# Joins of a triangular inverse in four corners, u transposed in one pass, and loads in halves at two positions, in a chunked attention with a gated MLP

## The chip, the core and the metric

The kernel runs on one core of a Trainium2 chip, in one launch. The metric is device time in microseconds. TensorE multiplies matrices into PSUM, VectorE (DVE), ScalarE (ACT) and GpSimd (POOL) work elementwise, and SyncE (SP) issues almost all DMAs. Each engine works through its own instructions in the order in which the program issues them, and waits on semaphores for the others.

## The reference, cut to what matters

Inputs: r, k, v, w, a, b of shape (4, 8, 768, 40), and the MLP's weights. A state of 40x40 per batch and head runs over 768 steps:

```
y[t]  = r[t] @ state
Sa    = state @ a[t]
state = state * w[t] - outer(Sa, b[t]) + outer(v[t], k[t])
```

y, with the heads side by side (width 320), goes through a gated MLP: `h = gelu(x @ w_in)` with 1024 columns, halves u and v, v normalised and mixed over time by a 768x768 matrix, and `x + (u * v) @ w_out`.

## The kernel before, in words

The recurrence is cut into 12 chunks (`c`) of 64 steps. In a chunk the steps depend on each other through a unit lower triangular 64x64 matrix for each of the 32 batch-head pairs; its inverse turns the chunk into matrix products. Work is done per chunk and half (`f` = 0, 1, two batches each).

The stages of one chunk, with lines of the listing:

- **gate** (338 to 397): VectorE scans the decays from tile `main` (two buffers, loaded by `load_main`, line 274), scales k, a and b, TensorE transposes (`kt`) and multiplies (`ab`, 384 to 386, on four tiles of 64x64, two PSUM banks), VectorE and ScalarE mask the results into `at` and `nts`.
- **inverse** (399 to 478): the 32x32 diagonal blocks of the inverse come from a substitution on GpSimd for two chunks at a time (`inv_load` copies a unit pattern out of `band`, `inv_sub` 415, `inv_end`, `inv_turn`, `inv_back`). The lower left corner is joined from them by two rounds of small matmuls: `inv_g` (452) writes PSUM tile `gp`, `post_g` (461) copies it to `gs`, `inv_x` (466) writes `xp`, `post_x` (475) copies it into `xt`. A round has 16 entries q and two halves h: 32 matmuls of 64 rows by 32 columns, each half on one tile of the array; a float32 matmul shows as two records in the trace.
- **chain** (499 to 633): with the state: `chain1` (`ru`), `chain2` (`us`), `post2` (u into the lower half of `vu`), `chain3` (`sp`, the new state), `copy3` (state to `vs`), `chain_u` (573, u transposed, `ut`), `post_u` (into `vut`), `chain4` (`pq`, from `rt` and `vut`), `chain5` (`yp`), `post5` and `store5` (y to DRAM tensor `xd`). `chain_t` transposes the state for `chain5` (`tp`).
- **loads**: `load_main`, `load_vb` (v for `chain1`), `load_vu` (a ScalarE copy into `vu`, 485) and `load_rv` (492, r and v transposed, into `rt` and `vut`) for later chunks, all on SyncE but `load_vu`.
- **fill** (911 to 945): parts of the MLP of earlier steps are done inside the attention, by loads of `xf` out of `xd`, a product `hf` and a store `hd`.

Every piece of work has a position in microseconds (constants `YC`, `CHAIN`, `YG`, `GATE`, `BACK` and others, lines 45 to 78; `at_` at 639). `in_order` (123) sorts the pieces by position and holds back those that would need a PSUM bank too early; the pieces are then issued in this order. The positions therefore set only the order on each engine and queue; the real times follow from waits. After chunk 11 the rest of the MLP runs.

Of the kernel before, what the change touches and what calls it, by code (L numbers as in the profile page):

```python
# [9 lines left out]
F32 = mybir.dt.float32  # L10
# [6 lines left out]
B, H, S, D = 4, 8, 768, 40  # L17
C = 64
NCH = S // C
NP = H // 2  # L20
DM = H * D
# [5 lines left out]
NQ = B * NP  # L27
# [13 lines left out]
LOADS = -12.0  # L41
PER = 25.258
LATE = 2.5
STORE = 1.5
GATE = ((-101.908, -100.107, -99.028, -96.184, -97.801, -95.604, -92.188, -90.251, -93.577, -91.478, -91.823),
    (-93.163, -92.271, -89.673, -85.987, -88.462, -85.151, -80.147, -78.616, -83.325, -79.712, -81.287))
GATE0 = {(0, 0): (-50.0, (0, 0.6, 1.2, 2.0, 2.1, 3.5, 5.0, 6.2, 6.1, 10.6, 7.4)), (0, 1): (-43.168, (-2.368, -1.768,
# [159 lines left out]
def engines(tc):  # L207
    nc = tc.nc
    return tuple(InOrder(tc, e) for e in (nc.vector, nc.scalar, nc.gpsimd, nc.tensor, nc.sync))
# [6 lines left out]
def attention(tc, a, xd, flag, keep, ps, mlp=None):  # L216
# [3 lines left out]
    V, A, G, T, Q = engines(tc)  # L220
    with ExitStack() as ctx:

        def pool(nm, side):

            c = ctx.enter_context(ExitStack())
            return c.enter_context(tc.tile_pool(name=nm, bufs=1, side=side)), c.close

        mlp.open_fill()
        st, _ = pool("at_static", "left")
# [4 lines left out]
        gt, gt_right = pool("at_gate", "right")  # L234
# [7 lines left out]
        def static(nm, n, shape, where=None):  # L242
            return [(where or st).tile(shape, F32, name=f"{nm}{i}") for i in range(n)]
# [6 lines left out]
        xts = static("xt", 2, [128, NQ, C])  # L250
        spare = gt.tile([128, 1], F32, name="spare")
        ident = st.tile([128, 128], F32, name="ident")
        mask = st.tile([128, C], F32, name="mask")
        band = st.tile([128, 128], F32, name="band")
        n = WU
        ones, rc, hsp = fixed[0][:, 0:n], fixed[0][:, n - C:2 * n - C], fixed[1][:, 0:n]
        nts = [p.tile([128, 2, NQ, C], F32, name=f"nts{i}") for i, p in enumerate((iw, iv))]
# [3 lines left out]
        gss = static("gs", 1, [128, 16, 32], iv)  # L261
        scs = static("sc", 2, [128, 2 * NP, C])
        rts = static("rt", 2, [128, 2, 4, C])
        call = keep.tile([128, NCH * B, NP], F32, name="call")
        vuts = static("vut", 2, [128, 2, 2, 4, C])
        vus = static("vu", 2, [128, 2 * DM + 24])

        exs = ring("ex", [128, 2, NP, C + 1])
        ats = ring("at", [128, 2, NP, 2, C], RING_AT)
# [1 line left out]
        def main_of(i):  # L271
            return mains[i % 2]

        def load_main(i):
            if i < 2 * NCH:
                for h in range(2):
                    Q.dma_start(out=main_of(i)[64 * h:64 * h + D], in_=a["main"][i, D * h:D * h + D])

        warm = gt.tile([128, 128], F32, name="warm")
        V.memset(warm, 0.0)  # L280
# [26 lines left out]
        def blanks():  # L307
            out = []
            for t in gss + scs:
                out.append(lambda t=t: G.memset(t, 0.0))  # L310
            for t in kbts:
                out.append(lambda t=t: G.memset(t[:, :, DM:DM + 24], 0.0))
            for t in vus:
                out.append(lambda t=t: G.memset(t[64:128, 2 * DM:2 * DM + 24], 0.0))
            return out

        def zeros():
# [15 lines left out]
        def nt_of(c):  # L333
            return nts[c // 2 % 2][:, c % 2]

        gate, kbs, unit, x1_of, st2, pqt, bk, xin, yts = {}, {}, {}, {}, {}, {}, {}, {}, {}
# [107 lines left out]
        def inv_back(c, k):  # L444
# [3 lines left out]
            else:  # L448
                r = slice(64 * (k - 1), 64 * (k - 1) + 32)
                A.copy(out=xt[r, :, 0:32], in_=xt[r, :, 32:64])  # L450

        def inv_g(c):
            nt, x1z = nt_of(c), x1_of[c]
            gp = bk["gp"] = ps("gp")
            for q in range(NQ):
                for h in range(2):
                    r = 64 * h
                    T.matmul(gp[r + 32:r + 64, 32 * q:32 * q + 32], lhsT=nt[r:r + 64, q, 32:64],
                             rhs=x1z[r:r + 64, q], start=True, stop=True, tile_position=(r, r + 32))

        def post_g(c):
            gs, gv = gss[0], bk.pop("gp").rearrange("p (q x) -> p q x", x=32)
            A.copy(out=gs[32:64], in_=gv[32:64])
            A.copy(out=gs[96:128], in_=gv[96:128])

        def inv_x(c):
            xt, gs = xts[c % 2], gss[0]
            xp = bk["xp"] = ps("xp")
            for q in range(NQ):
                for h in range(2):  # L470
                    r = 64 * h
                    T.matmul(xp[r:r + 32, 32 * q:32 * q + 32], lhsT=gs[r:r + 64, q],
                             rhs=xt[r:r + 64, q, 32:64], start=True, stop=True, tile_position=(r, r))

        def post_x(c):
            xt, xv = xts[c % 2], bk.pop("xp").rearrange("p (q x) -> p q x", x=32)
            A.copy(out=xt[0:32, :, 32:64], in_=xv[0:32])
            A.copy(out=xt[64:96, :, 32:64], in_=xv[64:96])


        def load_vb(c, f):
            if c < NCH:
                Q.dma_start(out=vss[f][0:64], in_=a["vb"][c, f])

        def load_vu(c, f):
            if c == 0:
                Q.dma_start(out=vus[f][0:64, 0:2 * DM], in_=a["vs"][0, f])
            elif c < NCH:
                A.copy(out=vus[f][0:64, 0:2 * DM].rearrange("p (g h x d) -> p g h x d", g=4, h=2, x=2),
                       in_=vss[f][0:64].rearrange("p i (g x) h d -> p (i g) h x d", x=2))  # L490

        def load_rv(c, f):
            if c < NCH:
                for x in range(2):
                    r = slice(64 * x, 64 * x + D)
                    Q.dma_start(out=rts[f][r], in_=a["rt"][c, f, x])
                    Q.dma_start(out=vuts[f][r, 0], in_=a["vt"][c, f, x])

        def chain1(c, f):
            at, vs = at_of(c, f), vss[f]  # L500
# [13 lines left out]
            return scs[f][:, :, 0:D]  # L514

        def vu_of(f):
            return vus[f][:, 0:2 * DM].rearrange("p (i g h x d) -> p i g h x d", i=2, g=2, h=2, x=2)

        def chain_t(c, f):
            if c:  # L520
# [20 lines left out]
        def post2(c, f):  # L541
            us, vu = bk.pop(("us", f)), vu_of(f)
            for h in range(2):
                for x in range(2):
                    A.mul(out=vu[64:128, :, :, h, x], in_=us[h][64 * x:64 * x + 64, 0:160].rearrange("p (i g d) -> p i g d", i=2, g=2), mul=-1.0)
# [26 lines left out]

        def chain_u(c, f):
            ut = bk["ut", f] = ps("ut")
            for j in range(16):
                r = 64 * (j % 2)
                T.matmul(ut[r:r + 64, C * (j // 2):C * (j // 2) + C], lhsT=vus[f][64:128, D * j:D * j + 64],
                         rhs=ident[64:128, 64:128], start=True, stop=True, tile_position=(64, r), skip_group_check=True)

        def post_u(c, f):  # L580
            e, ut = 64 + D, bk.pop(("ut", f))
# [53 lines left out]
        for f in range(2):  # L635
            load_vu(0, f)
        pieces = []

        def at_(p, f, *args, **kw):
            pieces.append((p, f, args, kw))  # L640

        for k, f in enumerate(blanks()):
            at_(BLANKS + 0.01 * k, f)
        for k, f in enumerate(zeros()):
            at_(ZEROS + 0.01 * k, f)
        for f in range(2):
            at_(LOADS, load_vb, 0, f)
            at_(LOADS, load_rv, 0, f)
        for c in range(NCH):
            for f in range(2):  # L650
                y, n = GATE0.get((c, f)) or (YG[c], GATE[f])
                at_(y + n[0], gate_1, c, f, 0)
                at_(y + n[1], gate_1, c, f, 1)
                at_(y + n[2], gate_2, c, f, E={"V": V, "G": G}[GATEE.get((c, f), GE)[0]])
                at_(y + n[3], gate_c, c, f)
                for i in range(2):
                    at_(y + n[4 + i], gate_3, c, f, i, E={"V": V, "G": G}[GATEE.get((c, f), GE)[1]])
                for g, p in zip((gate_t, gate_k, gate_s), n[6:]):
                    at_(y + p, g, c, f)
                for h in range(2):  # L660
                    at_(y + n[9] + 0.001 * h, gate_a, c, f, h)
                    at_(y + n[10] + 0.001 * h, gate_n, c, f, h)
                at_(y + n[5] + LATE, load_main, 2 * c + f + 2)
                z, n = YC[c], CHAIN0.get((c, f), CHAIN[f])
                for g, p in zip((chain1, post1, chain_t, post_t, chain2, post2, chain3, post3, copy3, chain_u, post_u, chain4, post4, chain5, post5), n):
                    at_(z + p, g, c, f)
                at_(z + n[14] + STORE, store5, c, f)
                at_(z + n[0] + LATE, load_vb, c + 1, f)
                at_(z + max(n[6], n[9]) + LATE, load_vu, c + 1, f)
                at_(z + n[13] + LATE, load_rv, c + 1, f)  # L670
            z = YC[c]
            for (g, *k), p in zip(((inv_back, 0), (inv_back, 1), (inv_back, 2), (inv_g,), (post_g,), (inv_x,), (post_x,)), BACK0.get(c, BACK)):
                at_(z + p, g, c, *k)
        for g in GROUPS:
            z, v = (0, INV0[g[0]]) if g[0] in INV0 else (YC[g[0]], INV)
            at_(z + v[0], inv_load, g)
            at_(z + v[1], inv_in, g)
            for s in range(31 - LAST):
                y = {}
# [601 lines left out]
```

## Time and profile before

| | us |
|---|---|
| median of three runs | 648.37 |
| lowest and highest | 646.72, 649.48 |
| profiled execution, its own time | 651.27 |
| its span in the trace | 649.5 |
| TensorE matmul busy, share of the span | 551.1, 85% |
| VectorE, GpSimd, ScalarE busy | 496.9, 370.0, 363.6 |
| mean granted share of TensorE's clock | 0.899 |

All times in the trace count from the start of the span. The time of an execution is a little longer than its span. A row of the chain names what the last work waited for, back to the start: start, duration and what; "issue" is time in which the engine waited for nothing that the profile shows. A row of a timeline or of the chain that merges records gives their number after an x.

### The profile page before, as it was taken

Reading aid. Unit: us, or ns where it says so; the run is one execution under the profiler, and the core shown is the slowest. Engines: PE = TensorE matmul, PEld = TensorE weight load, DVE = VectorE, ACT = ScalarE, POOL = GpSimd, SP = SyncE. Lnnn points to the kernel's source line nnn. Section 1 sums busy time; section 2 is a strip of 40 time slices with the busy share of each in tenths; the row PEclk is TensorE's granted clock in tenths of the full one; section 3 lists DMA queues with packets and bytes.
Section 4 is the critical chain, followed back from the end, with each engine's and each line's share of the span. In section 5 each row is a group of like instructions: output and inputs, shape, how many; then the busy total and the mean of one; then the engine's idle time right before and its main releaser. Section 6 shows DMA issues by size and latency. Waiting matters only on the chain.

```text
span 649.5 us, 25246 instructions
## 1 busy us (share of the span) xinstructions
PE 551.1 (85%) x10734; PEld 502.6 (77%) x10734; DVE 496.9 (77%) x954; ACT 363.6 (56%) x769; POOL 370.0 (57%) x600
## 2 busy tenths in 40 slices
PE   6438859768998798999998799698998998899896
PEld 5327758657887787888887687597998987899896
DVE  7767989699779566877799856748699799778943
ACT  3333957457877576787867678556345324625410
POOL 3485838816974844588389642656644632544331
PEclk8658877567999897999998899788999999999999
DMA  5443334243444353553354346337023541401001
GB/s 194 130 120 94 96 80 117 77 121 89 128 113 134 91 151 92 154 131 108 105 137 134 106 133 168 106 113 203 14 80 104 157 144 67 124 26 56 30 13 55
DMA packets 54945, 69.69 MB, mean 107 GB/s; under 512 B 21704, under 2 KB 39752, under 8 KB 52808
## 3 DMA queue, kind: packets, MB, share of 16 engines
q1 hardware_dynamic: 54824, 67.99, 36.8%
q8 instruction: 86, 1.41, 1.0%
q14 instruction: 35, 0.29, 0.1%
HBM read 54.86 MB, written 13.11 MB: 105 GB/s over the span
## 4 chain that ended last, share of the span: by engine, by line
PE 46%; DVE 26%; issue 10%; POOL 7%; ACT 6%; DMA 2%; SPq 1%; DVEq 0%; POOLq 0%; ACTq 0%
PE sg L202 7%; PE yp L202 5%; PE hf L202 4%; PE op L202 3%; DVE v L202 3%; PE sp L202 3%; PE ab L202 3%; PE pq L202 3%; PE ut L202 3%; PE ru L202 3%; DVE stg L202 3%; PE hu L202 3%; PE kt L202 2%; PE xp L202 2%; DVE p L202 2%
## 5 line engine op out<-in xcount | busy, mean ns | idle before, releaser
L202 POOL TENSOR_TENSOR tg<-x,n 128x135 f32<-128x135 f32 (+25 forms) x203 | 106.2, 523 | 98.1 <-ACT gs L202 40.0
L202 POOL TENSOR_TENSOR x<-x,tg 128x135 f32<-128x135 f32 (+25 forms) x203 | 108.2, 533 | 15.9
L202 PE MATMUL sg<-wsh,vh 128*128 128x384 f32 x192 | 65.9, 343 | 4.6 <-DVE y L202 3.9
L202 PE MATMUL sg<-wsh,vl 128*128 128x384 f32 x192 | 66.0, 344 | 3.5 <-POOL vl L202 3.5
L202 PE MATMUL sg<-wsl,vh 128*128 128x384 f32 x192 | 65.8, 343 | 1.7 <-DVE wsl L202 0.9
L202 ACT ACTIVATE nts<-ab 32x512 f32<-32x512 f32 x96 | 46.5, 484 | 28.2 <-PE ab L202 27.0
L202 PE MATMUL kt<-ident,kb 128*128 128x128 f32 x192 | 35.4, 333 | 27.4 <-DVE fixed L202 17.8
L202 POOL TENSOR_TENSOR gx<-g,gy 128x384 fp32r<-128x384 f32 x30 | 32.0, 1076 | 40.1 <-ACT gy L202 40.1
L202 PEld LDWEIGHTS kt<-ident,kb 128*128 128x128 f32 x192 | 26.7, 170 | 32.6 <-issue 26.7
L202 DVE TENSOR_TENSOR at<-ab,mask 64x512 f32<-64x512 f32 x48 | 31.8, 677 | 26.1 <-ACT nts L202 25.4
L202 POOL TENSOR_TENSOR rs<-rs,mhalf 128x1 f32<-128x1 f32 x24 | 14.7, 615 | 64.9 <-DVE rs L202 61.3
L202 ACT CAST vh<-v 128x512 fp32r<-128x512 f32 x24 | 14.6, 620 | 58.3 <-DVE v L202 58.3
L202 PE MATMUL ab<-at,kb 64*64 64x64 f32 x1536 | 39.6, 269 | 7.1 <-DVE fixed L202 6.2
L202 PEld LDWEIGHTS ab<-at,kb 64*64 64x64 f32 x1536 | 35.7, 179 | 10.1 <-issue 8.4
L202 ACT CAST gy<-g 128x384 fp32r<-128x384 f32 x30 | 15.3, 513 | 50.2 <-DVE g L202 50.2
L202 PEld LDWEIGHTS sg<-wsh,vh 128*128 128x128 f32 x192 | 36.5, 190 | 5.9 <-issue 2.6
L202 PEld LDWEIGHTS sg<-wsh,vl 128*128 128x128 f32 x192 | 36.6, 191 | 5.4 <-POOL vl L202 5.4
L202 PE MATMUL yp<-pqs,kbt 128*64 128x64 f32 x768 | 33.5, 249 | 7.8 <-ACT vs L202 3.4
L202 PEld LDWEIGHTS yp<-pqs,kbt 128*64 128x64 f32 x768 | 29.5, 159 | 11.6 <-ACT vs L202 3.6
L202 PEld LDWEIGHTS sg<-wsl,vh 128*128 128x128 f32 x192 | 36.5, 190 | 2.3 <-DVE wsl L202 1.2
L202 PE MATMUL sp<-vu,kbt 128*64 128x40 f32 x704 | 28.1, 237 | 11.6 <-issue 8.7
L202 DVE SCALAR_TENSOR_TENSOR g<-sg,gl,bt 128x384 f32<-128x384 f32 x32 | 19.5, 610 | 23.9 <-POOL gx L202 14.9
(158 smaller groups left out, 1609.2 us busy)
## 6 DMA issues: line engine op xcount, KB each, us to landing
main<-main SPq DMA_DIRECT2D x44, 321.4 KB
hd<-hv SPq DMA_DIRECT2D x20, 256.0 KB
v<-hd SPq DMA_DIRECT2D x20, 256.0 KB
vs<-vb SPq DMA_DIRECT2D x24, 160.0 KB
rt<-rt SPq DMA_DIRECT2D x48, 80.0 KB
vut<-vt SPq DMA_DIRECT2D x48, 80.0 KB
xd<-yt SPq DMA_DIRECT2D x96, 40.0 KB
ws<-seq_w SPq DMA_DIRECT2D x20, 192.0 KB
```

What stands on the lines that cost most here:

```text
L202: return self.tc.keep_in_program_order(f(*a, **k))
```

## The change

It has four parts. `inv_g` and `inv_x` put the entries q = 0 to 7 (`f` = 0) and 8 to 15 (`f` = 1) onto different columns of the array, so that consecutive matmuls go to four tiles; the PSUM tile has 256 columns instead of 512, and the posts copy it in four pieces of 32 partitions by 256 instead of two of 32 by 512. `chain_u` transposes two heads at a time out of a `vu` whose heads lie 64 apart instead of 40: 8 transposes instead of 16 matmuls. The two halves of a `main` load get positions of their own (from chunk 2 on, the second 4.6 or 3.4 later), and so do the two halves of a load of r and v (1.7 or 1.15 later). For the wider `vu`, `band` moves to the pool of the gate, and more of `vu` is cleared at the start.

```diff
+MAIN_GAP = (4.6, 3.4)
+RV_GAP = (1.7, 1.15)
...
-        band = st.tile([128, 128], F32, name="band")
+        band = gt.tile([128, 128], F32, name="band")
...
-        vus = static("vu", 2, [128, 2 * DM + 24])
+        vus = static("vu", 2, [128, 64 * 15 + D])
...
-        def load_main(i):
+        def load_main(i, h):
             if i < 2 * NCH:
-                for h in range(2):
-                    Q.dma_start(out=main_of(i)[64 * h:64 * h + D], in_=a["main"][i, D * h:D * h + D])
+                Q.dma_start(out=main_of(i)[64 * h:64 * h + D], in_=a["main"][i, D * h:D * h + D])
...
-                out.append(lambda t=t: G.memset(t[64:128, 2 * DM:2 * DM + 24], 0.0))
+                out.append(lambda t=t: G.memset(t[64:128, 0:960].rearrange("p (j x) -> p j x", x=64)[:, :, D:64], 0.0))
...
+        def corners():
+            return [(8 * f + j, 64 * h + 32 * f, 64 * h) for j in range(8) for f in range(2) for h in range(2)]
+
         def inv_g(c):
...
-            for q in range(NQ):
-                for h in range(2):
-                    r = 64 * h
-                    T.matmul(gp[r + 32:r + 64, 32 * q:32 * q + 32], lhsT=nt[r:r + 64, q, 32:64],
-                             rhs=x1z[r:r + 64, q], start=True, stop=True, tile_position=(r, r + 32))
+            for q, n, r in corners():
+                T.matmul(gp[n:n + 32, 32 * (q % 8):32 * (q % 8) + 32], lhsT=nt[r:r + 64, q, 32:64],
+                         rhs=x1z[r:r + 64, q], start=True, stop=True, tile_position=(r, n), skip_group_check=True)
 
         def post_g(c):
-            gs, gv = gss[0], bk.pop("gp").rearrange("p (q x) -> p q x", x=32)
-            A.copy(out=gs[32:64], in_=gv[32:64])
-            A.copy(out=gs[96:128], in_=gv[96:128])
+            gs, gv = gss[0], bk.pop("gp")[:, 0:256].rearrange("p (q x) -> p q x", x=32)
+            for f in range(2):
+                for r in (0, 64):
+                    A.copy(out=gs[r + 32:r + 64, 8 * f:8 * f + 8], in_=gv[r + 32 * f:r + 32 * f + 32])
...
+        def heads(f, r):
+            e = vus[f][r, 0:1]
+            return bass.AP(tensor=e.tensor, offset=e.offset, ap=[e.ap[0], [64, 16], [1, D]])
...
-        def load_rv(c, f):
+        def load_rv(c, f, x):
             if c < NCH:
-                for x in range(2):
-                    r = slice(64 * x, 64 * x + D)
-                    Q.dma_start(out=rts[f][r], in_=a["rt"][c, f, x])
-                    Q.dma_start(out=vuts[f][r, 0], in_=a["vt"][c, f, x])
+                r = slice(64 * x, 64 * x + D)
+                Q.dma_start(out=rts[f][r], in_=a["rt"][c, f, x])
+                Q.dma_start(out=vuts[f][r, 0], in_=a["vt"][c, f, x])
...
         def chain_u(c, f):
             ut = bk["ut", f] = ps("ut")
-            for j in range(16):
-                r = 64 * (j % 2)
-                T.matmul(ut[r:r + 64, C * (j // 2):C * (j // 2) + C], lhsT=vus[f][64:128, D * j:D * j + 64],
-                         rhs=ident[64:128, 64:128], start=True, stop=True, tile_position=(64, r), skip_group_check=True)
+            for j in range(8):
+                T.transpose(out=ut[0:64 + D, C * j:C * j + C], identity=ident[64:128, 64:128],
+                            in_=vus[f][64:128, 128 * j:128 * j + 64 + D])
...
-                at_(y + n[5] + LATE, load_main, 2 * c + f + 2)
+                for h in range(2):
+                    at_(y + n[5] + LATE + (MAIN_GAP[f] if h and c > 1 else 0), load_main, 2 * c + f + 2, h)
...
-                at_(z + n[13] + LATE, load_rv, c + 1, f)
+                for x in range(2):
+                    at_(z + n[13] + LATE + (RV_GAP[f] if x else 0), load_rv, c + 1, f, x)
```

`inv_x` and `post_x` change as `inv_g` and `post_g` do; `load_vu` and the operands of `post2` and `chain3` address `vu` through `heads`.

## Rows read from the trace of the kernel before

**Rows 1.** Busy time by stretch: us, each engine's busy time (records), PEclk, DMA share, GB/s

```profile
64.00:150.00 86.00, 64.21 (x1726) 57.58 (x1720) 74.86 (x151) 54.20 (x118) 50.66 (x98) 0.72 0.37 99
...
278.00:304.00 26.00, 24.02 (x740) 21.11 (x735) 17.62 (x34) 18.84 (x41) 22.85 (x37) 1.00 0.46 121
...
424.00:650.00 226.00, 207.34 (x1150) 197.97 (x1142) 169.81 (x315) 89.97 (x176) 103.40 (x96) 0.98 0.27 83
```

**Rows 2.** The chain that ended last, 150 to 320 us: start, us, what

```profile
161.51 0.45 PE us L202 x32
...
170.94 1.13 PE gp L202 x64
...
174.47 1.12 issue
...
192.32 1.67 PE yp L202 x64
194.00 0.93 PE ab L202 x64
...
217.82 3.78 issue
...
221.93 1.90 PE ut L202 x32
223.83 2.93 PE yp L202 x64
226.76 1.67 PE ab L202 x64
...
248.17 2.54 issue
...
281.05 1.08 PE ut L202 x32
...
294.93 1.31 issue
...
302.24 1.02 PE kt L202 x8
```

**Rows 3.** The page: busy by engine; the instruction DMA queue: packets, MB, share

```profile
PE 551.1 (85%) x10734; PEld 502.6 (77%) x10734; DVE 496.9 (77%) x954; ACT 363.6 (56%) x769; POOL 370.0 (57%) x600
...
q8 instruction: 86, 1.41, 1.0%
```

**Rows 4.** Timeline of SyncE's DMA issues, 120 to 300 us

```profile
212.96 0.71 SPq L202 DMA_DIRECT2D main<-main  x2
213.84 0.48 SPq L202 DMA_DIRECT2D vs<-vb  x1
...
242.88 0.71 SPq L202 DMA_DIRECT2D main<-main  x2
245.81 0.47 SPq L202 DMA_DIRECT2D vs<-vb  x1
```

**Rows 5.** Busy time by stretch, around the piece of issue at 217.82

```profile
213.00:219.00 6.00, 4.81 (x187) 4.41 (x183) 5.54 (x13) 4.80 (x13) 5.45 (x8) 1.00 0.78 191
222.00:228.00 6.00, 6.00 (x152) 5.76 (x156) 2.20 (x5) 1.28 (x2) 5.37 (x9) 0.50 0.04 8
```

**Rows 6.** The chain that ended last, 320 to 440 us

```profile
394.23 0.58 ACT gs L202
...
395.46 1.20 PE xp L202 x62
...
401.83 1.21 PE ut L202 x32
```

**Rows 7.** The chain that ended last, 60 to 150 us

```profile
65.82 0.58 ACT gs L202
...
91.61 1.92 PE gp L202 x64
```

**Rows 8.** Groups by shape, ScalarE: busy us, mean ns, idle before

```profile
L202 ACT ACTIVATE nts<-ab 32x256 f32<-32x256 f32 x48 | 18.1, 378 | 0.6
...
L202 ACT COPY gs<-gp 32x512 f32<-32x512 f32 x24 | 13.9, 578 | 0.6
```

**Rows 9.** Timeline, 231 to 237 us

```profile
233.21 1.18 ACT L202 COPY gs<-gp 32x512 f32<-32x512 f32 x2
...
234.57 0.88 PE L202 MATMUL xp<-xt,gs 64*32 64x32 f32 x44
```

More of the change, by code (lines that the diff above doesn't have):

```diff
@@ L468, in inv_x @@
             xp = bk["xp"] = ps("xp")
[L469 to L473, printed above, removed]
+            for q, n, r in corners():
+                T.matmul(xp[n:n + 32, 32 * (q % 8):32 * (q % 8) + 32], lhsT=gs[r:r + 64, q],
+                         rhs=xt[r:r + 64, q, 32:64], start=True, stop=True, tile_position=(r, n), skip_group_check=True)
         def post_x(c):
-            xt, xv = xts[c % 2], bk.pop("xp").rearrange("p (q x) -> p q x", x=32)
-            A.copy(out=xt[0:32, :, 32:64], in_=xv[0:32])
-            A.copy(out=xt[64:96, :, 32:64], in_=xv[64:96])
+            xt, xv = xts[c % 2], bk.pop("xp")[:, 0:256].rearrange("p (q x) -> p q x", x=32)
+            for f in range(2):
+                for r in (0, 64):
+                    A.copy(out=xt[r:r + 32, 8 * f:8 * f + 8, 32:64], in_=xv[r + 32 * f:r + 32 * f + 32])
         def load_vb(c, f):
@@ L483, in load_vb @@
                 Q.dma_start(out=vss[f][0:64], in_=a["vb"][c, f])
+        def heads(f, r):
+            e = vus[f][r, 0:1]
+            return bass.AP(tensor=e.tensor, offset=e.offset, ap=[e.ap[0], [64, 16], [1, D]])
         def load_vu(c, f):
             if c == 0:
-                Q.dma_start(out=vus[f][0:64, 0:2 * DM], in_=a["vs"][0, f])
+                Q.dma_start(out=heads(f, slice(0, 64)), in_=a["vs"][0, f].rearrange("s i g h x d -> s (i g h x) d"))
             elif c < NCH:
-                A.copy(out=vus[f][0:64, 0:2 * DM].rearrange("p (g h x d) -> p g h x d", g=4, h=2, x=2),
+                A.copy(out=heads(f, slice(0, 64)).rearrange("p (g h x) d -> p g h x d", g=4, h=2),
                        in_=vss[f][0:64].rearrange("p i (g x) h d -> p (i g) h x d", x=2))
-        def load_rv(c, f):
+        def load_rv(c, f, x):
             if c < NCH:
-                for x in range(2):
-                    r = slice(64 * x, 64 * x + D)
-                    Q.dma_start(out=rts[f][r], in_=a["rt"][c, f, x])
-                    Q.dma_start(out=vuts[f][r, 0], in_=a["vt"][c, f, x])
+                r = slice(64 * x, 64 * x + D)
+                Q.dma_start(out=rts[f][r], in_=a["rt"][c, f, x])
+                Q.dma_start(out=vuts[f][r, 0], in_=a["vt"][c, f, x])
         def chain1(c, f):
@@ L516, in vu_of @@
         def vu_of(f):
-            return vus[f][:, 0:2 * DM].rearrange("p (i g h x d) -> p i g h x d", i=2, g=2, h=2, x=2)
+            return heads(f, slice(0, 128)).rearrange("p (i g h x) d -> p i g h x d", i=2, g=2, h=2)
         def chain_t(c, f):
@@ L647, in attention @@
             at_(LOADS, load_vb, 0, f)
-            at_(LOADS, load_rv, 0, f)
+            for x in range(2):
+                at_(LOADS, load_rv, 0, f, x)
         for c in range(NCH):
@@ L669, in attention @@
                 at_(z + max(n[6], n[9]) + LATE, load_vu, c + 1, f)
-                at_(z + n[13] + LATE, load_rv, c + 1, f)
+                for x in range(2):
+                    at_(z + n[13] + LATE + (RV_GAP[f] if x else 0), load_rv, c + 1, f, x)
             z = YC[c]
```

## The prediction, before the changed kernel was run

> **What bounds the kernel now.** I read the stages first [rows 1]: each stretch's busy time per engine and the granted TensorE clock. Between 64 and 150 us VectorE is the busiest engine, with 74.86 of 86 us. In a middle stretch of 26 us TensorE has 24.02, at full clock, and no other engine has more than 22.85. From 424 us on only the gated MLP runs, 226 us that the change does not touch. Next, the chain of work that ended last [rows 2]. From 151 to 306 us, some six chunks, it is TensorE work almost alone, broken by pieces named "issue": time in which TensorE waited for nothing that the profile shows. There are eleven over 0.1 us in that stretch, 13.4 us together, from 1.12 us at 174.47 to 1.31 us at 294.93 [rows 2]. So in this stretch a microsecond saved on TensorE is saved at the end. Before and after it the chain changes between engines, and only blocks that lie on it count.
>
> What are the issue pieces? The page has a queue for instructions alone, with 86 packets, 1.41 MB [rows 3]: 16.4 KB each. TensorE has 10,734 matmul and as many weight-load records [rows 3]; 21,468 over 86 is about 250 to a packet. So these are TensorE's instructions coming in blocks, and a piece of issue is a block that came late. The two largest, 3.78 us at 217.82 and 2.54 us at 248.17 [rows 2], come about 5 us after both halves of main were issued together, at 212.96 and 242.88 [rows 4]. Around the first the DMA engines are 0.78 busy, against 0.46 in the quiet 26 us [rows 5, 1]. After it the clock is 0.50, that is 1.2 GHz, and all that follows takes longer: ut 1.90 us for 1.08, yp 2.93 for 1.67, ab 1.67 for 0.93 [rows 2, 5], 2.8 us in all. The Trainium skill (Runtime: NRT & Kernel Launch, Instruction fetch mechanics) has the same blocks, 16 KiB of 256 instructions, and calls crossing from one to the next mostly hidden; here the trace disagrees by 13.4 us.
>
> **u transposed in one pass.** A chain_u was 16 matmuls in 32 records, 1.08 us at full clock and 1.90 at half [rows 2]. It becomes 8 transposes of 104 columns, each moving 64. The nearest row is kt: 8 transposes with 128 weight columns and 128 moved take 1.02 us [rows 2]. If nothing shrinks with the size, the new block costs 1.02; if it goes with the columns moved, 0.51. I take the weights' columns, 104/128 of 1.02, which is 0.83, since every transpose loads weights of its own. That is 0.25 us less at full clock; at half, 0.83 x 1.90/1.08 = 1.46, or 0.44 less. On the chain between 151 and 306 stand 11 of the 24 blocks, 9 at full clock and 2 at half: 9 x 0.25 + 2 x 0.44 = 3.1. Three more stand on it elsewhere, the last at 401.83 [rows 6]: 0.9. **Sum -4.1 us**, ends -0.8 (14 x 0.06) and -8. The wider spacing of vu changes the strides of post2 and load_vu, not their element counts: nothing. The larger clearing of vu and its first load in short pieces lie in the first microseconds, ahead of the first substitution on GpSimd, before which no chain step can start: nothing, and a microsecond or two of DMA time without that cover.
>
> **Four corners.** gp and xp are 64 records of 32 columns on two tiles: 1.13 us at full clock, 17.7 ns each, and 1.92 at half [rows 2, 7]. Four tiles with the same records could halve this: 0.57. No gain is the other end. The rows on four tiles are us, 0.45 us for 32 records (14.1 ns), and ab, 0.93 for 64 (14.5 ns) [rows 2]; both have more columns, but no block in the trace is faster per record, so I take 14.1 x 64 = 0.90: 0.23 less. Eleven blocks lie on the chain of the TensorE stretch (5 gp, 6 xp), five outside (from gp at 91.61 to xp at 395.46 [rows 6, 7]). **Sum 16 x 0.23 = -3.7 us**, ends 0 and -10.
>
> The price is on ScalarE. post_g and post_x made two copies of 32x512, 0.578 us each: 1.16. They now make four of 32x256; the nearest row is nts in that shape, 0.378 [rows 8]: 1.51, so 0.36 more. Where the chain goes through ScalarE there (five posts, from gs at 65.82 to gs at 394.23 [rows 6, 7]) all of it shows: 1.8. In the TensorE stretch gs is hidden behind pq and ru: at 233.21 it takes 1.18 us, so it is done at 234.39, and xp starts at 234.57 [rows 9]. A cover of 0.18, less the 0.23 by which TensorE arrives sooner, leaves a wait of about 0.4. I count three such chunks, since in the others a late instruction block had delayed xp anyway: 1.2. post_x is covered by the tp and yp ahead of chain2 (a kt-sized 1.02 and 1.67 us [rows 2]); without them it would cost another 0.36 each time. **Sum +3.0 us**, ends 0 and +8.6 (24 x 0.36).
>
> **Instructions.** A chain_u had 32 matmul records and 32 weight loads; 8 and 8 remain if one transpose is one record, as in kt, where 8 are 8. That is 48 x 24 = 1,152 fewer, 4.6 of 86 blocks, and 96 of the 1,475 records in the 26 us of rows 1, 6.5%. The nine smaller pieces of issue are 13.4 - 3.78 - 2.54 = 7.1 us; 6.5% of them is 0.5. Denser gp and xp ask for blocks faster, so I take no more. **-0.5 us**, ends 0 and -7.1.
>
> **The loads.** In SyncE's queue the second half of main's load for f = 0 moves behind load_vb of f = 1 (planned 4.2 later, the half 4.6), for f = 1 behind store5 and the next hd store. load_vb waits for chain1: it issued 0.9 us after main at 213.84 and 2.9 us after it at 245.81 [rows 4]. So the halves part by about 1 to 3 us, and an instruction block can pass between them. Behind the new wait stand the half itself and the load of x; main's next scan is a chunk away, some 26 us, and load_vb now issues one DMA sooner. The second half of r and v moves behind store5, four issues that wait for post5. chain4 of the next chunk needs it, again most of a chunk later: nothing. What the parting is worth: the first large piece with its slow clock cost 3.78 + 2.8 = 6.6 us, the second 2.54 + 2.8 = 5.4 (the same blocks follow it). I take half of the 12.0, as if one of the two went: **-6.0 us**. Ends -12.0 and +6.6, one more such piece, since each block boundary moves and may fall upon a half.
>
> **The sum.** -4.1 - 3.7 + 3.0 - 0.5 - 6.0 = -11.3 us. The profiled execution took 651.27 us, 2.9 over the median of 648.37, by about half of one such piece. 651.27 - 11.3 = 640.0 us, 1.3% under the median.
>
> **Rivals.** *The loads do not part the traffic.* The half follows load_vb at once (0.9 us in one of two), and the block is as late as before. Then the loads' term is 0: 651.27 - 5.3 = 646.0, no change against the median. For it: the bytes are the same. Against it: the 2.9 us in the other.
> *Both large pieces go and transposes cost by columns moved*: another 6 us from the loads and 3 of u's 4 to its end: 631. For it: there is no third piece of that size.
> *The corners run one after another, and four copies become the wait.* gp and xp keep 1.13 us, and every post costs its 0.36: +8.6, with -4.1 and -0.5: +4.0, 655.3, slower. It decides where gs ends after xp could start, at all 24 posts instead of eight. The cover of 0.18 us [rows 9] speaks for it; that the chain names ScalarE at few posts speaks against. The Trainium skill (TensorEngine Tiling (Array Packing), Gotcha 1: PSUM Pressure) says that different row tiles cannot write one PSUM bank at the same time, and gp is one bank; by that its corners would gain nothing. The trace speaks against it: kt alone on the array takes 127 ns for 128 columns, 32 for each 32, while gp's two row tiles, on one bank already, take 17.7 [rows 2].
>
> **How the numbers follow.** Chances: the forecast 0.58, the loads without effect 0.18, both pieces gone 0.15, the slower one 0.09. The range, 631 to 649.5 us, holds the first three and leaves out the last. A measurement can tell about 0.5%, 3.2 us, from no change: faster, below 645.1, is the first and third, 0.73; the same 0.18; slower 0.09.
>
> **What would show it.** Right: ut as 8 records of about 0.83 us; gp and xp near 0.90; ScalarE's gs at four copies of 0.37; two fewer microseconds of issue per large piece, and no half clock between 151 and 306 us; main's two issues apart with vs between. Wrong: ut at 1.02 or more, gp still at 1.13 with xp waiting for gs in every chunk, or issue over 13 us in the stretch.

## The result, and the profile after

Five runs of the changed kernel had a median of 641.03 us, beside 649.39 for the kernel before; the ratio is 0.985, 95% interval 0.981 to 0.990. The ratio counts for each kernel only the runs within 1.5% of its fastest, which leaves out two of the five of the changed kernel (647.72 and 650.87); over all runs the means have a ratio of 0.991. The forecast was 640.0, faster. Two later series of twelve runs each gave 0.984 and 0.989 (below). The executions of one kernel scatter: 23 of the kernel before, on one chip, took 640.42 to 658.26 us. A part worth half a per cent can therefore be seen in a trace but hardly in the times.

The execution profiled with the result took 650.87 us, far over the median. The trace shown below is that of `after_third`, a later run of the same changed kernel: 642.36 us, span 640.5. First the page, busy time by engine and the instruction queue (packets, MB, share):

```profile
PE 540.6 (84%) x10158; PEld 488.5 (76%) x10158; DVE 497.3 (78%) x954; ACT 370.0 (58%) x817; POOL 371.4 (58%) x600
...
q8 instruction: 82, 1.34, 0.9%
```

TensorE has 576 matmul records and as many weight loads fewer than in [rows 3], 1,152 in all as the prediction had it, and 82 instruction blocks instead of 86. ScalarE has 48 instructions more: two copies more in each of 24 posts.

Where did the time go? Busy time by stretch, of the kernel before (columns as in [rows 1]) ...

```profile
150.00:306.00 156.00, 141.74 (x4378) 126.87 (x4378) 114.39 (x217) 113.89 (x243) 110.91 (x189) 0.94 0.45 120
...
425.00:650.00 225.00, 206.34 (x1130) 197.23 (x1128) 169.32 (x314) 89.28 (x175) 103.12 (x95) 0.99 0.27 84
```

... and of the changed kernel:

```profile
150.00:306.00 156.00, 143.39 (x4328) 125.57 (x4326) 121.50 (x228) 123.64 (x279) 112.05 (x192) 0.93 0.44 123
...
416.00:641.00 225.00, 207.67 (x1130) 198.89 (x1128) 169.04 (x314) 89.37 (x175) 103.32 (x95) 0.98 0.26 84
```

The last 225 us hold the same 1,130 matmul records in both, only 9 us earlier: the MLP did not change, and the gain lies ahead of it. In the middle stretch VectorE and ScalarE have about 7 and 10 us more in the same 156 us: more of the work fits in, and ScalarE has the added copies besides. The granted clock is no better, 0.93 for 0.94. The gain can be placed more closely by the starts of gp: from the fifth chunk's to the seventh's it is 64.0 us before and 53.4 now, and these are the chunks in which the two large pieces of issue stood.

The chain of the changed kernel in that stretch, the lines that answer to [rows 2], and the new ones among them:

```profile
189.84 0.58 PE ut L204 x8
190.42 1.67 PE yp L204 x64
...
194.88 2.01 DVE x1z L204
...
198.30 0.75 ACT kbt L204 x2
199.07 0.62 ACT xt L204
...
199.71 0.36 ACT gs L204
...
200.10 0.37 ACT gs L204
200.49 0.36 ACT gs L204
...
200.87 0.37 ACT gs L204
...
201.29 0.34 PE xp L204 x17
...
208.39 0.58 PE ut L204 x8
...
240.20 1.33 issue
...
243.58 2.94 PE yp L204 x64
...
267.90 0.17 issue
...
302.42 0.39 DVE x L204 x2
```

ut takes 0.58 us instead of 1.08. No piece of issue is over 1.33 us here; before, two were 3.78 and 2.54. That is not so in every trace of the changed kernel: the one taken with the result has this piece,

```profile
245.91 2.43 issue
```

and that of `after_again` one of 2.16 us. The pieces over 0.1 us sum to 14.1, 10.9 and 9.7 us in the three traces, where it was 13.4 in the one before. Half clock is still there too: yp takes 2.94 us at 243.58, behind the piece of 1.33, and 1.67 at full clock. And a stretch that was TensorE alone now goes again and again through the end of the substitution (x1z), ScalarE's copies and the four copies of gs before xp goes on.

The lines that answer to [rows 4], SyncE's issues: the halves of these two loads of main now stand 3 us apart, with the load for chain1 between them.

```profile
209.69 0.30 SPq L204 DMA_DIRECT2D main<-main  x1
212.19 0.47 SPq L204 DMA_DIRECT2D vs<-vb  x1
212.72 0.51 SPq L204 DMA_DIRECT2D main<-main  x1
...
235.10 0.30 SPq L204 DMA_DIRECT2D main<-main  x1
237.65 0.47 SPq L204 DMA_DIRECT2D vs<-vb  x1
238.18 0.51 SPq L204 DMA_DIRECT2D main<-main  x1
```

Last, the timeline of the join in one chunk, as [rows 9], with gp ahead of it:

```profile
222.70 0.76 PE L204 MATMUL gp<-x1z,nts 64*32 64x32 f32 x64
224.62 1.53 ACT L204 COPY gs<-gp 32x256 f32<-32x256 f32 x4
...
225.72 0.87 PE L204 MATMUL xp<-xt,gs 64*32 64x32 f32 x26
226.21 0.27 PEld L204 LDWEIGHTS xp<-xt,gs 64*32 64x32 f32 x20 [0.26 <-ACT gs L204]
```

gp is done at 223.5, but ScalarE comes to gs only at 224.62 and is done with it at 226.15. xp begins at 225.72 with what is there and waits; it gets going at 226.21.

### The profile page after: what moved, and what is told of

It reads as the page before. It is cut to its first block, busy times and chain, and to the rows that moved or that the text cites. A ratio compares the mean times of both kernels' runs of the same rounds, so it can differ in the third digit from the quotient of the medians.

```text
span 649.1 us, 24143 instructions
## 1 busy us (share of the span) xinstructions
PE 545.0 (84%) x10158; PEld 491.5 (76%) x10158; DVE 495.6 (76%) x954; ACT 370.5 (57%) x817; POOL 368.4 (57%) x600
## 4 chain that ended last, share of the span: by engine, by line
PE 44%; DVE 30%; issue 9%; ACT 9%; POOL 6%; DMA 2%; SPq 0%; DVEq 0%; ACTq 0%; POOLq 0%
PE sg L204 10%; PE yp L204 5%; PE hf L204 4%; PE op L204 3%; PE sp L204 3%; PE ab L204 3%; DVE v L204 3%; DVE stg L204 3%; PE hu L204 3%; DVE fixed L204 3%; DVE at L204 2%; DVE p L204 2%; PE kt L204 2%; DVE kb L204 2%; POOL tg L204 2%
## 5 line engine op out<-in xcount | busy, mean ns | idle before, releaser
L204 POOL TENSOR_TENSOR tg<-x,n 128x135 f32<-128x135 f32 (+25 forms) x203 | 104.0, 512 | 96.0 <-DVE n L204 49.6
L204 PE MATMUL pq<-rt,vut 40*64 40x64 f32 x1536 | 32.8, 229 | 4.2 <-ACT vut L204 1.5
L204 POOL TENSOR_TENSOR vl<-v,vh 128x512 fp32r<-128x512 f32 x24 | 31.5, 1319 | 8.2 <-ACT vh L204 8.2
```

Source lines behind the costliest of these rows:

```text
L204: return self.tc.keep_in_program_order(f(*a, **k))
```

## The experiments

Each was timed in five rounds beside the kernel before, unless said otherwise.

### Three parts alone

`u_only`: before with the new `chain_u` and the wider `vu`.

> Before with chain_u as 8 transposes alone (and the wider vu). Theory (u's block is TensorE work on the chain): the block takes 0.58 us at full clock and 1.02 at half as in the changed kernel, against 1.08 and 1.90, so 14 blocks x 0.5 on the chain are 7 us: 642. Rival (the instruction blocks that come late set the pace of this stretch, and the time saved in u turns into waits for them): 646 to 649, with the pieces of issue between 150 and 306 us over 15 us.

Measured: 644.07 us, ratio 0.987 (0.977 to 0.997). Faster, as the theory had it, by 2 to 15 us. The pieces of issue of 0.3 us and more between 150 and 306 us sum to 13.7 us, against 13.1 before: in these two traces the instructions saved took none of these waits away, and the shorter block added little.

`corners_only`: before with the joins in corners and the four copies.

```diff
+            for q, n, r in corners():
+                T.matmul(gp[n:n + 32, 32 * (q % 8):32 * (q % 8) + 32], lhsT=nt[r:r + 64, q, 32:64],
...
+                    A.copy(out=gs[r + 32:r + 64, 8 * f:8 * f + 8], in_=gv[r + 32 * f:r + 32 * f + 32])
```

> Before with the joins in four corners and the four copies alone. Theory (gp and xp gain 0.43 us each, but TensorE then waits for four copies of gs in every chunk, which gives most of it back): 646 to 649, gp at about 0.70, a wait for gs before xp in every chunk. Rival 1 (the gain is kept): 16 blocks x 0.43 = 7 us, 642. Rival 2 (copies cost more than the corners bring): 652 and above.

Measured: 651.04 us beside 651.44, ratio 1.000 (0.996 to 1.005): nothing, though gp is as short as in the changed kernel. Its chain:

```profile
214.47 3.06 issue
...
226.72 0.69 PE gp L202 x50
...
228.57 0.36 ACT gs L202
...
228.96 0.37 ACT gs L202
...
229.35 0.36 ACT gs L202
...
229.73 0.37 ACT gs L202
...
230.15 0.52 PE xp L202 x36
...
285.35 2.94 issue
```

In this chunk what gp saves ends in the wait for gs, which lies on the chain. The theory asked for such a wait in every chunk, and that did not come. What the weight loads of xp waited for (us in all, times, the longest), before and here:

```profile
PEld xp L202 <- ACT gs L202: 7.5, 7, 2.5
...
PEld xp L202 <- ACT gs L202: 7.6, 15, 2.8
```

These waits fall into 4 of the 12 joins before and 6 here, and sum to the same. The trace has another candidate: its pieces of issue over 0.1 us sum to 16.4 us instead of 13.4, and four are over 2 us, the largest 3.06 and 2.94. That denser blocks ask for instructions sooner would fit, but single traces of one kernel differ by more than these 3 us. Where the gain went is not shown.

`loads_only`: before with both gaps.

```diff
+                at_(y + n[5] + LATE + (MAIN_GAP[f] if h and c > 1 else 0), load_main, 2 * c + f + 2, h)
...
+                at_(z + n[13] + LATE + (RV_GAP[f] if x else 0), load_rv, c + 1, f, x)
```

> Before with the halves of main, r and v at two positions alone. Prediction's theory (an instruction block can pass between the halves, and one of the two large pieces of issue with the half clock behind it goes): 6 us, 643. Rival (as many pieces of issue, only elsewhere, as the changed kernel's trace has some 12 us of them between 160 and 306): 647 to 650.

Measured: 642.45 us, ratio 0.989 (0.980 to 0.998): some 7 us. The pieces of issue of 0.3 us and more sum to 9.7 us, and these are the largest:

```profile
196.98 1.37 issue
...
278.69 1.10 issue
```

And its busy time by stretch shows the clock:

```profile
150.00:306.00 156.00, 145.97 (x4662) 129.81 (x4664) 121.72 (x227) 121.03 (x258) 109.25 (x189) 0.98 0.47 126
```

No piece over 2 us is left, and the granted clock in the stretch is 0.98 instead of 0.94. In the same 156 us TensorE gets through 4,662 matmul records instead of 4,378. From the fifth chunk's gp to the seventh's it is 55.4 us, where it was 64.0 before and 64.6 in corners_only. So parting the loads takes the large pieces away; both went in this trace, not one of two.

The DMA packets recorded in the traces show how. In the kernel before, the 80 packets of main's two halves run from 214.16 to 218.87 us; the next instruction packet starts at 218.84, 7.7 us after the one ahead of it where 4.1 is the median of the stretch, and takes only 1.27 us; TensorE goes on at 221.60, the end of the largest piece. At the second piece main's last packet starts at 247.72 and the instruction packet at 247.77. All nine pieces of 0.3 us and more in the stretch end 1.4 to 1.7 us after an instruction packet has landed. In loads_only the first half of a load starts its packets from 236.60 to 238.00, an instruction packet starts at 238.09, and the second half follows from 240.48: the block passes between the halves.

`after_again`, the changed kernel on the same chip:

> The changed kernel as it is, beside the parts on the same chip, and a second trace of it: 637 to 642. The parts should sum to it if they are independent: u about -7, corners about -1, loads 0 to -6.

Measured: 641.52 us, ratio 0.984 (0.980 to 0.989). The parts give -1.3, 0.0 and -1.1%, and together -2.4%, against -1.6% for the whole. With the width of these intervals that is no contradiction, nor does it show that the parts simply add.

### The burst doubled, and r and v alone

`main_extra`, timed once:

```diff
                     Q.dma_start(out=main_of(i)[64 * h:64 * h + D], in_=a["main"][i, D * h:D * h + D])
+                    Q.dma_start(out=mlp.dump[i, D * h:D * h + D], in_=a["main"][i, D * h:D * h + D])
```

> Before, with each half of a load of main followed by a copy of the same size into DRAM that nothing uses: the traffic of main doubled, no other work. Theory (an instruction block that stands behind main's load comes late and the clock falls to half): issue between 150 and 306 us goes from 13 us to 20 or more, with four or more pieces over 2 us, and the time to 655 to 670. Rival (late blocks come from TensorE asking too fast, not from the loads): pieces of issue as before, time within 3 us of before.

Measured: 658.02 us, where the runs of before around it had a median of 654.28, from 643.54 to 663.00. Issue in the stretch sums to 17.3 us, more than the 13.4 of before but under the 20 that the theory asked for, and two pieces, not four, are over 2 us (2.76 and 3.56). The direction is the theory's, the size is not, and one run does not carry more.

`rv_only`: before with RV_GAP alone, MAIN_GAP at zero.

```diff
+MAIN_GAP = (0.0, 0.0)
+RV_GAP = (1.7, 1.15)
```

> Before with the halves of r and v alone at two positions, main's halves together. Theory (main's burst is what an instruction block stands behind): no change against before, within 0.5%, with a piece of issue over 2 us left in the stretch from 150 to 306 us. Rival (any shorter burst helps): 643 to 646.

Measured: 651.85 us, ratio 1.010 (1.006 to 1.014): slower, which neither theory had. Over all runs of both kernels the ratio of the means is 1.006, so the size is half a per cent to one. Its chain has three pieces over 2 us:

```profile
220.23 2.90 issue
...
248.02 2.82 issue
...
290.31 2.03 issue
```

The queue shows where the second half went:

```profile
210.45 1.77 SPq L204 DMA_DIRECT2D xd<-yt  x4
212.33 0.30 SPq L204 DMA_DIRECT2D rt<-rt  x1
212.69 0.64 SPq L204 DMA_DIRECT2D vut<-vt  x1
213.42 0.36 SPq L204 DMA_DIRECT2D hd<-hv  x1
213.88 1.59 SPq L204 DMA_DIRECT2D main<-main  x2
```

The second half of r and v now comes right ahead of the hd store and both halves of main, so the burst in front of an instruction block has become longer: main's packets there run from 215.67 to 221.68 us, 6.0 us instead of the 4.7 before. The pieces of issue over 0.1 us sum to 13.3 us, no more than before, and the granted clock of the stretch is 0.91 instead of 0.94. That the order is the cause of the loss is argued from these lines, not shown. That main's gap, not r's and v's, brings the gain of loads_only follows from the two ratios.

### Less of the change, and more of it

`no_corners`: the changed kernel with the joins as before.

> The changed kernel with the joins as before: u in one pass and the loads in halves alone. Theory (the corners give TensorE 0.43 us a block and take it back at the wait for the four copies of gs): 640 to 642, as the changed kernel. Rival 1 (they bring what TensorE gains): 645 to 648. Rival 2 (they cost): 636 to 638.

Measured: 643.13 us, ratio 0.994 (0.988 to 1.000). The changed kernel did not run beside it; on the same chip, in the series of after_again, it took 641.52 us. Over all runs the means have a ratio of 0.987 here and 0.985 for after_again, so the corners' share cannot be told from zero here either.

`x_corner`: only inv_x and post_x in corners.

> The changed kernel with inv_g and its two copies as before, inv_x in four corners. Theory (the wait for gs is what eats the gain, and the four copies of post_x are covered): gs two copies of 0.58, a wait of under 0.3 us before xp in most chunks, and 1 to 3 us less than the changed kernel: 638 to 640. Rival (gs is late because ScalarE is busy before it, whatever the number of copies): no change.

Measured: 642.72 us, ratio 0.993 (0.987 to 0.999), beside the same runs as no_corners and not under the 641.52 of after_again. In the trace gs is two copies again and is done sooner after gp, but ScalarE starts it as late as ever, 1.92 us after gp begins at 223.31 as at 222.70 in the changed kernel: the rival's reading fits as well.

`late7`: one load's second half moved behind the load that waits for chain1.

```diff
-                    at_(y + n[5] + LATE + (MAIN_GAP[f] if h and c > 1 else 0), load_main, 2 * c + f + 2, h)
+                    at_(y + n[5] + LATE + (6.6 if h and (c, f) == (2, 1) else MAIN_GAP[f] if h and c > 1 else 0), load_main, 2 * c + f + 2, h)
```

> The changed kernel, with the second half of one load of main (for chunk 3, f = 1, planned at 5.58) moved to 8.78, behind the load of v for chunk 1 that waits for chain1. In the changed kernel both halves of it are still issued together, at 60.5 us, and an instruction block comes 3 us late at 65. Theory (that block stands behind the load): the piece of issue at 65 falls below 1.5 us, and 2 to 3 us of the time go: 638. Rival (the block is late for another reason, or the chain does not hang on it): no change against the changed kernel.

In the changed kernel this piece is in the timeline, ahead of the rest of a chain1:

```profile
65.39 0.54 PE L204 MATMUL ru<-vs,at 64*64 64x40 f32 x11 [3.09 <-issue]
```

and in late7:

```profile
66.08 0.59 PE L204 MATMUL ru<-vs,at 64*64 64x40 f32 x11 [2.00 <-issue]
```

Measured: 642.53 us, ratio 0.991 (0.986 to 0.996). The wait fell by 1.1 us, not below 1.5, and the time shows nothing of it. By this pair of traces the load in front of the block is part of the cause, no more.

`late7_x`, both edits, and `after_third`, the changed kernel beside it:

> The changed kernel with the one load of main later and inv_g with its two copies as before: both edits of the last runs that shortened a wait in the trace. Theory (each takes a wait off the chain): no piece of issue over 2 us before 150 us, two copies of gs, and 636 to 640, 2 to 5 us under the changed kernel beside it. Rival (what they free is taken up by later waits between 306 and 424 us, where TensorE does not set the pace): as the changed kernel within 2 us.

> The changed kernel once more, as the measure beside late7_x on the same chip: 638 to 642.

Measured: 638.30 us, ratio 0.988 (0.982 to 0.993), and 640.39 us, 0.989 (0.985 to 0.993). The piece over 2 us before 150 us is gone, the longest there is 1.68, and the median is 2.1 us lower; but the intervals overlap, and no difference can be told.

`no_rv_gap`: late7_x with r and v together again.

> late7_x with the halves of r and v issued together again, as before the change; main's halves stay apart. rv_only measured r and v in halves at 1% slower alone. Theory (it is the order of r and v behind store5 that costs, whatever main does): 632 to 636. Rival (it cost there because main's whole burst came right behind; with main in halves it costs nothing): as late7_x, 637 to 641.

Measured: 639.02 us, as late7_x. Its ratio, 0.980 (0.974 to 0.986), is the lowest of all, but against runs of before with a median of 655.04 on that chip, and its interval overlaps late7_x's. Whether r and v in halves cost anything once main is in halves stays open, and no version is shown to be faster than the changed kernel.

## Why the prediction was right, point by point

**The bound** held: the gain lies ahead of the MLP, and TensorE's stretch in the middle was the place. That pieces of issue are instruction blocks kept waiting by main's load is borne out by loads_only, which moves nothing but loads: no large piece left, clock 0.98, and an instruction packet between the halves. The rival that the loads do not part the traffic fell with it, at least for this kernel. The second rival, both large pieces gone, is what loads_only and the trace shown have, but the time did not go to 631, and the two other traces of the changed kernel keep a piece of 2.43 and of 2.16 us. Part of what TensorE saved went into waits for ScalarE and for the substitution: TensorE's idle time before gp for x1z rose from 5.4 to 8.9 us, and to 7.4 and 7.3 in the other two traces.

**u in one pass** was right in sign and mis-sized. I had 0.83 us a block from the weights' columns; it takes 0.58. The end that goes by the columns moved, 0.51, was nearer. 14 blocks x 0.5 are 7 us instead of the 4.1 of the sum; u_only's 2 to 15 us allow both. The instruction term, -0.5, was too small to be told: the pieces of issue rose by 0.6 us in u_only's trace.

**The corners** were mis-sized in the gain and right in the price. gp takes 0.76 us in the timeline, where the kernel before has

```profile
231.29 1.20 PE L202 MATMUL gp<-x1z,nts 64*32 64x32 f32 x64
```

so 0.44 less, nearly twice my 0.23. The copies cost what the nts row said: 0.364 each in the groups by shape, 1.53 us for four. The waits of the changed kernel for gs:

```profile
PEld xp L204 <- ACT gs L204: 10.6, 20, 3.1
PE xp L204 <- ACT gs L204: 6.1, 3, 3.0
```

TensorE's weight loads for xp waited 3.1 us more than the 7.5 of before, against the +3.0 of the sum. The 20 times are not 20 chunks, since a join can now wait once for each copy: they fall into 7 joins, three of them between 160 and 306 us, as I had counted (four in the two other traces, where the waits sum to 10.7 and 9.3 us). That the totals agree is in part luck, for outside the stretch the added waits stand at other posts than the five I named.

With 0.44 a block and 3.1 us of waits the corners should have brought 16 x 0.44 - 3.1 = some 4 us; corners_only measured 0 within 0.5%. My -0.7 us lies within that, but not for the reason given: the gain was larger than I thought and did not show in the time, and why it did not stays open. The slower rival had gp keep its 1.13 us and the copies become the wait at every post: neither happened. The rule that I weighed there, that two row tiles cannot write one PSUM bank together (the Trainium skill, TensorEngine Tiling (Array Packing), Gotcha 1: PSUM Pressure), does not hold back this shape: gp is one bank still, and its 64 records now take 0.76 us.

**The loads** were -6.0, and loads_only's ratio makes it about 7, between 1 and 13. The mechanism held, but one sign that I had named did not come: there is still half clock between 151 and 306 us in the changed kernel, 0.93 for 0.94 over the stretch, although the term counted 2.8 us of slow clock for each piece. loads_only alone has 0.98. Another sign, issue over 13 us as a mark of being wrong, did come in the trace taken with the result (14.1), though not in the other two. My sentence on r and v, "nothing", was not argued well enough: alone they cost half a per cent to one. I asked only who needs the data, not what the moved DMAs would then stand in front of. With main in halves too, as in the change, no_rv_gap could not tell a cost, so for the change itself it stays open.

**The sum** of -11.3 us set against the profiled execution gave 640.0; by the ratio (0.981 to 0.990) the changed kernel is 7 to 12 us under before. That it was so near is partly luck: u brought more than its term, the parts measured alone sum to 2.4%, some 15 us, and the whole gave less than that sum. The added waits for the substitution account for some of the difference; the rest is not shown.

## What to carry to other kernels

Where TensorE stands still for nothing that the profile names, look at what the DMA engines carry at that moment: its own instructions come by DMA, and a large load issued in one go can delay them; here TensorE stood still for up to 3.78 us, with half clock behind it. Parting the load by something that waits helped here, by about 1%; a moved DMA must be priced by what it then stands in front of, not only by when its data are needed. Before a matmul is made faster, look at what follows it: gp became 0.44 us shorter, its result came in four copies instead of two, and no run shows a gain.

## What the runs showed of the hardware that was not expected

Eight transposes with 104 weight columns and 64 moved take 0.58 us at full clock and 1.02 at half (at 167.01 us in the chain of another trace of the changed kernel), against 1.02 and 1.90 for 128 and 128: nearer to the ratio of the columns moved (0.51) than to that of the weights (0.83). The rows halved as well, from 128 to 64, so which of the two it goes by is not shown. On four tiles 64 records of 32 columns take 0.76 us, under 12 ns each, faster than any block before the change (14.1). TensorE went on 1.4 to 1.7 us after a block of its instructions had landed, in all nine pieces of issue of 0.3 us and more in the stretch. And two DMAs of 80 KB for each half chunk, moved by a few places in a queue, cost half a per cent to one of the kernel's time; why is not shown.
